# Gated mix of an FFT filter and a Mish MLP on one core: other queues and slices for the first loads, and a new order of the tasks

## The chip, the cores and the metric

The kernel runs on one core of a Trainium2 chip. The metric is the device time of one execution in microseconds (us): before, 133.72 us in the median of three runs (133.17 to 134.02). The core has five engines with queues of their own: TensorE (PE; its weight loads are listed as PEld), VectorE (DVE), ScalarE (ACT), GpSimd (POOL) and SyncE (SP), which only issues transfers. Transfers are issued by SP and ACT, each on a queue of its own, and are carried by 16 shared DMA engines.

## The reference, cut to what matters

```python
x = A_x                                            # 1 x 2048 x 512, bf16
g = sigmoid((x * gate_w).sum(-1, keepdims=True))
X = rfft2(x) * (A_w_r + 1j * A_w_i)                # filter: 2048 x 257, two parts
a = irfft2(X)
h = x @ w1 + b1                                    # w1: 512 x 1792, the same x
act = h * tanh(softplus(h))                        # Mish
b = act @ w2                                       # w2: 1792 x 512
return g * a + (1 - g) * b
```

Two branches read the same x: a two-dimensional Fourier filter, and an MLP with the Mish function. A gate for each row mixes them.

## The kernel before, in words

x is kept as 16 tiles of 128 rows. The program is a list of named tasks, each with its engine and what it reads and writes; a string, ORDER, gives the order of the tasks on each engine (`name:engine:slot`, where the slot is a bank of PSUM for PE's tasks, or a scratch buffer). Every engine works through its own tasks in that order and waits by semaphore for what a task needs. A task that waits holds up all that is behind it on its engine. Tasks that two numbers name belong to a chunk (four tiles of x) or a tile and a part.

The tasks, by the stage they belong to:

- Loads. `x0`, `x2` (two tiles each, 256 KB), `x4`, `x8`, `x12` (four tiles, 512 KB); `w1_0`, `w1_2`, `w1_6`: slices of w1 by columns (2, 4 and 8 of the 14 column tiles of 128); `gw`: the gate weights, one row read 128 times into all partitions; `cRF`, `cFD`, `inv`, `rft`, `edge`, `ldM0..3`, `ldG0..3`: constants of the Fourier stages; `braw`: the bias; `w2_*`: slices of w2. `wr..s..` and `wi..s..` (for instance `wr0s1`): the rows of the filter into a staging area, in ten loads, each into 16 partitions; of each half one load takes 32 rows as they lie, one takes 31 or 32 rows in reversed order, and for the first half one takes a single row.
- PE warm-up. `warm` (14 matmuls of 256 columns on constants) and the fillers `fl0`, `fl1`, `fl2` (3, 8 and 5 matmuls of 128 columns, whose results nobody reads).
- `tr`: transposes a tile of x on PE; `evx` evicts it (ACT or DVE). `tr_b`, `ev_b`: the same for the bias.
- `bf` (DVE): sums and differences of the halves of x. `p`, `d`, `t`, `it`, `id`, `ip`: the matrix stages of the forward and inverse transform on PE; `ep`, `ed`, `et`, `eit`, `ec`, `ey` evict them. `sh` and `hx` are copies between the stages, inside SBUF.
- `gt` (DVE): the gate's dot product, one for each tile, with `gw`; `zcl`, `ez`, `ez1`, `omg`, `gc`: the sigmoid.
- `wrm`, `wim`, `win`, `wrn`, `wrc`, `wic`, `wrz`, `wiz`: bring the filter from the staging area into its final place (mostly DVE). `p2`, `p1`, `ad` (DVE): multiply by the filter. `e1`, `xp2`, `xp1`, `ead`, `e2`, `e3`: a correction for the edge frequencies between the filter and the inverse transform; all of `it` comes after `e3`.
- `m<chunk>_<ft>` (mm1): four matmuls of 512 columns into one PSUM bank; `h<chunk>_<ft>` (ACT): Mish of it. `n<tile>` (mm2): 14 matmuls into one bank. `o` and `s`: scale and add the two branches into the result; `out`: stores. The last tile, 15, is made in two halves of 256 columns.

A PSUM bank is taken again only when its last reader is done. mm1 of chunk 0 needs `evx0` to `evx3` and a slice of w1; mm1 and mm2 need nothing of the Fourier branch, so ORDER strews them between its stages. The lines of the profile: L463 is the helper that issues every transfer, L475 the one that evicts; L488 warm-up, L498 fillers, L544 `tr`, L567 `p`, L581 `d`, L666 `t`, L740 `it`, L764 `id`, L799 `ip`, L788 mm1, L792 Mish, L815 mm2, L557 `bf`, L589 `gt`, L630 and L631 `wrm`/`wim`, L699 `e1`, L804 and L805 `o`, L809 `s`. Tensors: rA holds x at first, w_sb are w1, w2 and small constants kept in w2's place, rS is the staging area of the filter, ps is PSUM.

Of the kernel before, what the change touches and what calls it, by code (L numbers as in the profile page):

```python
# [309 lines left out]
bf8_1:dve gt4:dve m0_11:pe:3 h0_11:act m1_8:pe:6 h1_8:act tr11:pe:7 evx11:act m0_7:pe:2  # L310
h0_7:act m1_10:pe:6 h1_10:act bf12_1:dve tr9:pe:7 evx9:dve p8:pe:0 p9:pe ep8:act
m0_9:pe:2 tr8:pe:3 p10:pe:4 bf12_0:dve p11:pe p12:pe:0 p13:pe p14:pe:6 p15:pe
h0_9:act ep10:act ep12:act gt5:dve ep14:dve m1_6:pe:2 h1_6:act m0_10:pe:4 h0_10:act
d6:pe:0 evx8:dve gt6:dve gt7:dve gt8:dve d7:pe tr10:pe:2 d4:pe:6 d5:pe
tr12:pe:3 m1_12:pe:4 evx12:dve ed3:act gt9:dve m0_13:pe:5 ed2:act tr15:pe:3 d2:pe:0
d3:pe h1_12:act h0_13:act ed1:act evx15:dve gt10:dve gt11:dve evx10:act d0:pe:6
d1:pe d14:pe:4 d15:pe m1_11:pe:3 m0_8:pe:0 ed0:act ed7:act m1_0:pe:2 tr14:pe:1
h0_8:act h1_11:act wi0s1:sp wi0s2:sp evx14:act wr0s1:sp wr0s0:sp wr1s1:sp wr1s0:sp
wrm001:dve wrm010:dve gt12:dve gt13:dve gt14:dve wrm100:dve d8:pe:4 d9:pe m0_6:pe:6
m1_9:pe:3 tr13:pe:7 gt15:dve wip0:pool wip1:pool ed4:act h1_0:act h0_6:act evx13:dve  # L320
m0_4:pe:1 d12:pe:4 d13:pe m1_1:pe:2 h0_4:act h1_9:act ed6:act h1_1:act d10:pe:0
d11:pe m1_5:pe:3 ed5:act m1_7:pe:4 wi0s0:sp m2_8:pe:2 m0_12:pe:5 m3_11:pe:0 wi1s1:sp
sh0_3:sp sh0_0:sp wim011:dve sh0_2:sp h1_5:act ldM0:sp wim111:dve wrm000:dve wim100:dve
wrm110:dve wim101:dve zcl:dve sh0_1:sp wim110:dve m3_0:pe:3 wrm011:dve t1_0:pe:6 wrm101:dve
wrm111:act h1_7:act t1_1:pe wim000:dve wim001:dve wim010:dve m3_10:pe:4 et1:act win0:dve
h3_0:act h0_12:act m3_2:pe:1 t0_0:pe:6 t0_1:pe et0:dve wic0:dve win1:dve m3_9:pe:3
m1_13:pe:5 wiz0:dve p20_0:dve:0 p21_0:dve:1 h3_2:act h3_11:act h3_10:act ez:pool ldM1:sp
t3_0:pe:0 t3_1:pe sh1_0:sp sh1_2:sp sh1_3:sp sh1_1:sp h1_13:act et3:act m2_10:pe:4
h2_10:act h2_8:act m2_9:pe:5 h2_9:act h3_9:act m2_12:pe:0 t2_0:pe:6 t2_1:pe m2_6:pe:1
m2_4:pe:3 wrn01:sp wrn00:sp et2:act p20_1:dve p21_1:dve p23_0:dve:2 p23_1:dve h2_4:act  # L330
m3_4:pe:6 ldM3:sp t6_0:pe:4 wrc0:dve wrz0:dve p1_3:dve ez1:dve omg:dve ad_3:dve
p1_1:dve t6_1:pe h2_12:act et6:act p1_0:dve wic1:dve t7_0:pe:2 t7_1:pe m2_7:pe:0
et7:act h2_7:act m2_11:pe:7 ldM2:sp wrn10:sp t5_0:pe:4 wiz1:pool ad_0:dve ad_1:dve
t5_1:pe m2_2:pe:2 h2_2:act et5:act wrn11:sp wrc1:dve m3_3:pe:0 m3_6:pe:3 m2_3:pe:2
t4_0:pe:4 t4_1:pe p27_0:dve:0 wrz1:dve p26_0:dve:1 h3_6:act h3_3:act et4:act m3_7:pe:3
m2_1:pe:0 h2_1:act h2_6:act h2_11:act m3_8:pe:4 m3_12:pe:5 m2_13:pe:1 m3_1:pe:7 p22_0:dve:2
p27_1:dve p22_1:dve p1_7:dve p26_1:dve p1_6:dve ad_7:dve h3_12:act h2_13:act p1_2:dve
p25_0:dve:0 ad_6:dve w2_9:sp w2_4:sp w2_0:sp p24_0:dve:1 n5_0:pe:5 h3_8:act h3_7:act
h3_1:act h3_4:act p25_1:dve p24_1:dve ad_2:dve p1_5:dve ad_5:dve edge:sp ldG0:sp
p1_4:dve ad_4:dve o5_0:dve n6_0:pe:3 o6_0:act h2_3:act e1:pe:5 gc:dve xp20:dve:0  # L340
xp21:dve xp1:dve:1 rft:sp ldG3:sp ead:dve:2 m2_5:pe:6 m2_0:pe:7 h2_5:act h2_0:act
inv:sp ldG1:sp e2:pe:2 m3_13:pe:3 e3:dve ldG2:sp it1_0:pe:0 it1_1:pe eit1:dve
it5_0:pe:4 it5_1:pe h3_13:act eit5:act m3_5:pe:7 h3_5:act it2_0:pe:2 it2_1:pe it7_0:pe:0
eit2:act it3_0:pe:4 it3_1:pe it7_1:pe eit7:act eit3:act n4_0:pe:7 it0_0:pe:0 it4_0:pe:2
it0_1:pe it6_0:pe:4 it6_1:pe it4_1:pe eit6:act eit4:act eit0:dve hx8_0:act hx4_1:act
hx8_1:act o4_0:act hx0_0:act n0_0:pe:6 n2_0:pe:2 n3_0:pe:7 id10:pe:0 id11:pe id8:pe:4
hx4_0:act ec10:dve:0 ey10_1:dve ey10_0:dve id9:pe ec8:act:1 hx12_0:act o2_0:act o0_0:act
ey8_0:dve ey8_1:dve n1_0:pe:3 id6:pe:0 ip9:pe:6 o1_0:act o9:act id4:pe:4 ip10:pe:2
id5:pe id7:pe ec6:act:0 ip8:pe:3 ip11:pe:6 hx0_1:sp hx12_1:sp o3_0:dve o11:dve
ec4:act:1 o8:act n7_0:pe:7 ey6_1:dve ey6_0:dve o10:act ip6:pe:6 ip7:pe:0 ey4_0:dve  # L350
id2:pe:2 ey4_1:dve ip4:pe:1 id0:pe:4 id1:pe id3:pe ec0:act:0 o7_0:act s6:dve
ec2:act:1 s4:dve ey0_0:dve n11_0:pe:6 ey0_1:dve s7:dve ey2_1:dve id12:pe:0 ip0:pe:7
ip5:pe:4 id13:pe n10_0:pe:5 s11_0:dve s5:dve s0:dve ey2_0:dve ip3:pe:4 id14:pe:2
id15:pe ip1:pe:7 ec12:act:0 out5:act out7:act ec14:act:1 ey12_1:dve ey12_0:dve ip12:pe:6
ip2:pe:0 n8_0:pe:1 s1:dve ey14_0:dve ey14_1:dve ip13:pe:7 ip15:pe:2 n9_0:pe:3 s3:dve
s8_0:dve s10_0:dve ip14:pe:1 out11:sp out1:sp s2:dve o12:dve n12_0:pe:6 s12_0:dve
n13_0:pe:0 o13:dve s13_0:dve s9_0:dve o14:dve out13:act o15:act out3:act out9:sp
n15_256:pe:7 n14_0:pe:6 s14_0:dve out14:act s15_256:dve out15_256:sp n15_0:pe:1 s15_0:dve out15_0:act
"""


def _build(nc, A_x, A_w_r, A_w_i, B_x, B_w1, B_b1, B_w2, gate_w, out, XTP=16, LATE=8, NWARM=14,
           W1P=((0, 2), (2, 6), (6, 14)), XP=((0, 2), (2, 4), (4, 8), (8, 12), (12, 16)), SH=2):
    cs = _build_consts()
    d_front = nc.inline_tensor(_bf16_bits(cs["front"]), name="c_front").bitcast(BF)
    d_inv = nc.inline_tensor(_bf16_bits(cs["inv"]), name="c_inv").bitcast(BF)
# [4 lines left out]
    G = _Graph()  # L371
    es = ExitStack()
    with es:
# [100 lines left out]
        def evac(name, o, i, n, reads, writes, cls, engs=("act", "dve"), deps=()):  # L474
            fns = dict(dve=lambda e: e.tensor_copy(out=o(), in_=i()), act=lambda e: e.activation(o(), i(), AF.Copy))  # L475
# [410 lines left out]
```

## Time and profile before

| | |
|---|---|
| median of three runs | 133.72 us |
| the profiled execution: its time | 134.83 us |
| the profiled execution: its span | 133.2 us |
| PE busy | 127.2 us (95%) |
| DVE busy | 87.9 us (66%) |
| ACT busy | 77.4 us (58%) |
| moved by DMA | 20.28 MB, mean 152 GB/s |
| granted TensorE clock | 1.00 throughout |

The span runs from the first instruction to the last; the time of the execution has 1.6 us more around it. All times inside the kernel are counted from the start of the span. Matmuls overlap, so a single one is listed with 379 ns although the next one starts sooner; their rate is read from the chain of waits. In the chain, "issue" is time in which an engine waited for nothing that the profile shows. A row of the waits gives total us, number of times, and the longest.

### The profile page before, as it was taken

Reading aid. Unit: us, or ns where it says so; the run is one execution under the profiler, and the core shown is the slowest. Engines: PE = TensorE matmul, PEld = TensorE weight load, DVE = VectorE, ACT = ScalarE, POOL = GpSimd, SP = SyncE. Lnnn points to the kernel's source line nnn. Section 1 sums busy time; section 2 is a strip of 40 time slices with the busy share of each in tenths; the row PEclk is TensorE's granted clock in tenths of the full one; section 3 lists DMA queues with packets and bytes.
Section 4 is the critical chain, followed back from the end, with each engine's and each line's share of the span. In section 5 each row is a group of like instructions: output and inputs, shape, how many; then the busy total and the mean of one; then the engine's idle time right before and its main releaser. Section 6 shows DMA issues by size and latency. Waiting matters only on the chain.

```text
span 133.2 us, 2246 instructions
## 1 busy us (share of the span) xinstructions
PE 127.2 (95%) x901; PEld 71.5 (54%) x901; DVE 87.9 (66%) x162; ACT 77.4 (58%) x110; POOL 5.4 (4%) x13
## 2 busy tenths in 40 slices
...
GB/s 100 145 351 407 307 205 170 172 56 0 245 270 199 219 229 238 220 259 359 348 316 1 0 0 5 0 241 310 74 9 0 0 58 99 0 162 0 0 236 79
DMA packets 12533, 20.28 MB, mean 152 GB/s; under 512 B 1324, under 2 KB 6956, under 8 KB 12460
## 3 DMA queue, kind: packets, MB, share of 16 engines
...
q14 instruction: 2, 0.02, 0.0%
...
## 4 chain that ended last, share of the span: by engine, by line
PE 58%; DVE 30%; DMA 6%; issue 4%; SPq 1%; DVEq 0%
PE ps L815 32%; PE ps L788 14%; DVE tmp L679 7%; DMA w_sb<-in_B_w_dram 6%; DVE rC L684 4%; DVE rC L687 4%; PE ps L740 3%; PE ps L764 3%; PE ps L799 3%; PE ps L567 2%; DVE w_sb L589 2%; DVE rW L630 2%; DVE rA L630 2%; DVE rA L640 2%; PE ps L544 2%
## 5 line engine op out<-in xcount | busy, mean ns | idle before, releaser
L788 PE MATMUL ps<-rX,w_sb 128*128 128x512 bf16 x224 | 51.9, 379 | 1.7 <-DMA w_sb<-in_B_w_dram 1.7
L788 PEld LDWEIGHTS ps<-rX,w_sb 128*128 128x128 bf16 x224 | 20.8, 98 | 23.3 <-issue 1.9
L815 PE MATMUL ps<-w_sb,hs 128*128 128x512 bf16 x112 | 25.0, 379 | 0.0
L792 ACT ACTIVATE hs<-ps,b1f 128x512 bf16<-128x512 f32 x28 | 18.5, 696 | 3.4 <-PE ps L788 3.2
L815 PEld LDWEIGHTS ps<-w_sb,hs 128*128 128x128 bf16 x112 | 10.8, 98 | 12.4
L475 ACT ACTIVATE rC<-ps 128x1024 bf16<-128x1024 f32 x13 | 13.2, 1031 | 1.2 <-PE ps L567 0.7
L815 PE MATMUL ps<-w_sb,rD 128*128 128x512 bf16 x56 | 12.7, 379 | 0.0
L557 DVE TENSOR_TENSOR rB<-rA 128x1024 bf16<-128x1024 bf16 (+1 forms) x10 | 5.5, 580 | 11.0 <-DMA rA<-in_A_x_dram 11.0
L815 PE MATMUL ps<-w_sb,rS 128*128 128x512 bf16 (+1 forms) x70 | 12.3, 336 | 0.0
L809 DVE SCALAR_TENSOR_TENSOR rX<-ps,omg,rX 128x512 bf16<-128x512 f32 (+1 forms) x9 | 5.9, 689 | 9.3 <-PE ps L815 9.3
L475 ACT ACTIVATE tmp<-ps 128x512 f32<-128x512 f32 x7 | 4.1, 597 | 13.4 <-PE ps L764 13.3
L589 DVE SCALAR_TENSOR_TENSOR w_sb<-rA,w_sb 128x512 bf16<-128x512 bf16 x16 | 11.0, 687 | 0.3
L792 ACT ACTIVATE rD<-ps,b1f 128x512 bf16<-128x512 f32 x14 | 9.1, 698 | 3.1 <-PE ps L788 3.1
L679 DVE TENSOR_TENSOR tmp<-rC,rA 64x1024 bf16<-64x1024 bf16 x16 | 10.6, 686 | 0.4
L804 ACT ACTIVATE rX<-ps,gcol 128x512 bf16<-128x512 f32 x4 | 2.6, 690 | 14.0 <-DVE rX L809 14.0
L774 DVE TENSOR_TENSOR rA<-tmp,ps 128x512 bf16<-128x512 f32 x16 | 10.0, 679 | 0.4 <-ACT tmp L475 0.4
L815 PEld LDWEIGHTS ps<-w_sb,rS 128*128 128x128 bf16 x70 | 6.8, 98 | 5.5
L792 ACT ACTIVATE rS<-ps,b1f 128x512 bf16<-128x512 f32 x14 | 9.0, 696 | 0.7 <-PE ps L788 0.3
L815 PEld LDWEIGHTS ps<-w_sb,rD 128*128 128x128 bf16 x56 | 5.4, 98 | 6.1
L804 ACT ACTIVATE rX<-ps,omg 128x512 bf16<-128x512 f32 x6 | 4.0, 685 | 7.4 <-PE ps L815 5.1
L475 ACT ACTIVATE rD<-ps 128x1024 bf16<-128x1024 f32 x8 | 8.0, 1035 | 0.0
L475 ACT ACTIVATE rF<-ps 128x1024 bf16<-128x1024 f32 x6 | 5.8, 1029 | 2.2 <-PE ps L740 2.2
...
## 6 DMA issues: line engine op xcount, KB each, us to landing
...
rF<-c_m SPq DMA_DIRECT2D x4, 512.0 KB, 6.3
rB<-c_g SPq DMA_DIRECT2D x4, 512.0 KB, 6.1
rA<-in_A_x_dram SPq DMA_DIRECT2D x3, 512.0 KB, 13.9
...
w_sb<-in_B_w_dram SPq DMA_DIRECT2D x2, 512.0 KB, 10.0
```

The costliest lines, as they stand in the source:

```text
L475: fns = dict(dve=lambda e: e.tensor_copy(out=o(), in_=i()), act=lambda e: e.activation(o(), i(), AF.Copy))
L557: return e.tensor_tensor(out=xu[:, a:b_, uv, :], in0=x_sb[:, a:b_, 0:256], in1=x_sb[:, a:b_, 256:512], op=ALU.add if uv == 0 else ALU.subt ...
L589: t_gt.append(dve(f"gt{t}", "gate", "stt", 512, lambda e, t=t: e.scalar_tensor_tensor(out=junk, in0=x_sb[:, t, :], scalar=1.0, in1=gwr, op ...
L630: return e.tensor_copy(out=o_, in_=i_)
L679: return e.tensor_tensor(out=zv(z)[lo], in0=Y[hi, f0:f0 + 8, :], in1=Wi[hi, f0:f0 + 8, 0:128], op=ALU.mult)
L684: return e.tensor_tensor(out=Y[:, f0:f0 + 8, :], in0=Y[:, f0:f0 + 8, :], in1=Wr[:, f0:f0 + 8, 0:128], op=ALU.mult)
L774: return e.tensor_tensor(out=yb[:, t:t + 2, 256 * h:256 * h + 256].rearrange("p t (i e) -> p t i e", e=2), in0=t4(z), in1=o4(bank(b, 1)), ...
L788: ins = e.matmul(bank(b), w1_sb[:, dt_, 128 * ft:128 * (ft + 1)], xT[:, c, dt_, :, :], start=(dt_ == 0), stop=(dt_ == 3))
L792: G.add(f"h{c}_{ft}", "mish", dict(act=lambda e, c=c, ft=ft, b=b: e.activation(hs[c][:, ft, :], bank(b), AF.Mish, bias=b1f[:, ft:ft + 1])) ...
L804: f_a = lambda e: e.activation(o_()[0], o_()[1], AF.Copy, scale=o_()[2])
L809: dve(name, "fin", "psums", hi - lo, lambda e: e.scalar_tensor_tensor(out=bs[:, t, lo:hi], in0=bank(b)[:, 0:hi - lo], scalar=col[:, t:t + ...
L815: ins = e.matmul(bank(b)[:, 0:hi - lo], hs[c][:, ft, 128 * tl:128 * (tl + 1)], w2_sb[:, ft, lo:hi], start=(ft == 0), stop=(ft == NFT - 1))
```

## The change

The gate weights are loaded as one row (`gwl`) into one partition, spread over all partitions by a product with a column of ones on PE (`gwb`), and evicted (`gwe`). w1 comes in slices of 4, 5 and 5 column tiles (`w1_0`, `w1_4`, `w1_9`). The filter loads read their rows in rising order as one line of memory for each partition, and what was reversed on the reading side is reversed on the writing side. Two of the three fillers go. The last tile of the result is made in 384 and 128 columns instead of 256 and 256. ORDER is new: all filter loads are on SP, while `w1_9`, `x12`, `cFD`, `ldM0` to `ldM2` and two `sh` copies are on ACT.

```diff
@@ -295,72 +295,72 @@
@@ ORDER (of the old one the first 9 and the last 2 lines) @@
-FILL = (3, 8, 5, )
+FILL = (3, )
...
-warm:pe:0 wrp0:pool ebase:pool ones:pool wrp1:pool ident:pool cRF:act braw:act x0:sp
-fl0:pe:1 tr0:pe:0 x2:sp w1_0:sp w1_2:sp bf0_0:dve bf0_1:dve bf2_1:dve x4:sp
-tr1:pe:1 gw:act tab:act bf2_0:dve evx1:dve fl1:pe:2 tr2:pe:2 evx0:act tr3:pe:3
-evx2:act tr_b:pe:0 p0:pe:4 p1:pe p2:pe:6 ep0:act evx3:dve ev_b:dve fl2:pe:2
-m0_1:pe:0 m0_0:pe:1 p3:pe w1_6:sp x8:sp x12:sp h0_1:act wi1s0:act wr0s2:sp
-bf4_1:dve bf4_0:dve m0_3:pe:0 m0_2:pe:4 m0_5:pe:5 ep2:act h0_0:act h0_2:act tr5:pe:1
-h0_3:act evx5:act tr6:pe:4 evx6:dve tr4:pe:6 tr7:pe:7 evx7:act cFD:sp evx4:dve
-p4:pe:2 p5:pe p6:pe:0 p7:pe h0_5:act ep6:act m1_4:pe:7 m1_3:pe:6 h1_3:act
-gt0:dve ep4:dve gt1:dve gt2:dve m1_2:pe:2 gt3:dve h1_2:act h1_4:act bf8_0:dve
...
-n13_0:pe:0 o13:dve s13_0:dve s9_0:dve o14:dve out13:act o15:act out3:act out9:sp
-n15_256:pe:7 n14_0:pe:6 s14_0:dve out14:act s15_256:dve out15_256:sp n15_0:pe:1 s15_0:dve out15_0:act
+warm:pe:0 cRF:act wrp0:pool ebase:pool ones:pool wrp1:pool ident:pool braw:act x0:sp
+bf0_1:dve fl0:pe:1 tr0:pe:0 bf0_0:dve x2:sp gwl:act tab:act bf2_0:dve evx0:act
+tr1:pe:1 evx1:act tr2:pe:2 tr3:pe:3 gwb:pe:0 p0:pe:4 evx2:act gwe:act bf2_1:dve
+evx3:dve w1_0:sp x4:sp w1_4:sp x8:sp p2:pe:6 p3:pe p1:pe tr_b:pe:2
+ev_b:dve gt0:dve gt1:dve gt2:dve m0_2:pe:2 m0_0:pe:3 bf4_0:dve tr4:pe:0 ep2:act
+ep0:act h0_2:act evx4:dve bf4_1:dve tr5:pe:2 m0_3:pe:4 tr7:pe:5 tr6:pe:0 h0_0:act
+w1_9:act evx5:act gt3:dve x12:act cFD:act evx6:act p4:pe:6 p5:pe p6:pe:2
+p7:pe ep6:act gt4:dve m0_7:pe:1 h0_7:act m0_4:pe:0 h0_4:act evx7:dve m1_4:pe:5
+gt5:dve tr9:pe:1 m1_0:pe:0 h0_3:act evx9:act h1_4:act h1_0:act bf8_0:dve bf8_1:dve
+p8:pe:2 m1_5:pe:1 h1_5:act p9:pe ep4:dve m1_11:pe:0 m1_8:pe:1 p10:pe:4 tr11:pe:6
+p11:pe h1_11:act ep8:act gt6:dve gt7:dve gt8:dve ep10:act m0_6:pe:0 wi0s0:sp
+wr0s1:sp bf12_0:dve bf12_1:dve p12:pe:2 p13:pe h1_8:act h0_6:act p14:pe:4 p15:pe
+ep14:act m1_9:pe:7 wi0s2:sp wr0s0:sp wr0s2:sp gt9:dve evx11:dve h1_9:act ldM1:act
+tr12:pe:0 ldM0:act evx12:act m1_1:pe:1 h1_1:act ep12:dve d2:pe:2 d4:pe:4 d3:pe
+m1_13:pe:7 d5:pe wrm001:dve h1_13:act gt10:dve ed1:dve ed2:dve m1_6:pe:0 h1_6:act
+wr1s1:sp wr1s0:sp d10:pe:2 d0:pe:6 d1:pe wi1s0:sp d11:pe ldM2:act ed5:act
+d6:pe:4 d7:pe tr15:pe:0 m0_8:pe:1 wrm011:dve evx15:dve ed0:dve wi1s1:sp wi0s1:sp
+ed3:act h0_8:act m1_2:pe:2 d14:pe:4 m0_11:pe:3 sh0_2:act gt11:dve wrm101:dve gt12:dve
+d15:pe ed7:act m1_7:pe:1 tr8:pe:0 h0_11:act sh0_1:act h1_2:act tr10:pe:6 wrm000:dve
+wrm111:dve m1_10:pe:7 tr13:pe:3 d8:pe:4 d9:pe evx13:act ed4:act evx8:dve gt13:dve
...
+h3_3:act h3_4:act t1_0:pe:2 t1_1:pe m2_6:pe:5 m3_9:pe:4 m2_0:pe:0 m3_13:pe:1 sh1_0:sp
...
+et4:act w2_4:sp w2_0:sp n2_0:pe:1 h3_1:act omg:dve p24_0:dve:2 h3_11:act o2_0:act
+n4_0:pe:3 h3_2:act m2_10:pe:2 p24_1:dve ad_5:dve p27_1:dve p1_7:dve p1_4:dve ad_4:dve
+edge:sp ad_7:dve e1:pe:1 xp20:dve:0 xp21:dve xp1:dve:1 o4_0:dve inv:sp n6_0:pe:4
...
+ip11:pe:5 ip12:pe:4 n12_0:pe:6 ip0:pe:2 o12:act s13_0:dve s7:dve o11:dve s3:dve
+s0:dve out1:act ip2:pe:1 ip5:pe:7 s5:dve s2:dve out3:act out7:sp n15_0:pe:3
+ip14:pe:1 n8_0:pe:7 s11_0:dve s15_0:dve s12_0:dve out15_0:sp out13:sp s8_0:dve out5:act
+o14:act out9:act out11:act n14_0:pe:6 s14_0:dve out14:act n15_384:pe:7 s15_384:dve out15_384:sp
...
-           W1P=((0, 2), (2, 6), (6, 14)), XP=((0, 2), (2, 4), (4, 8), (8, 12), (12, 16)), SH=2):
+           W1P=((0, 4), (4, 9), (9, 14)), XP=((0, 2), (2, 4), (4, 8), (8, 12), (12, 16)), SH=2):
...
@@ -511,7 +511,7 @@
         dma("cRF", RF, d_front[:, 0, :], kb=32, writes=["cRF"])
         dma("braw", brw, B_b1.rearrange("(ft p) -> ft p", p=128), kb=4, writes=["braw"])
         dma("cFD", FD.rearrange("p c m -> p (c m)"), d_front[:, 1:5, :].rearrange("p c m -> p (c m)"), kb=128, writes=["cFD"])
-        dma("gw", gwr, gate_w.unsqueeze(0).to_broadcast([128, 512]), kb=128, writes=["gw"])
+        dma("gwl", junk[0:1, :], gate_w.unsqueeze(0), kb=1, writes=["gwl", "junk"])
         for a, b_ in XP:
             dma(f"x{a}", x_sb[:, a:b_, :], xv[:, a:b_, :], kb=128 * (b_ - a), writes=[("x", t) for t in range(a, b_)])
         for a, b_ in W1P:
@@ -522,14 +522,17 @@
                 sg = stg[64 * ri + 32 * fh:64 * ri + 32 * fh + 32]
                 c0_ = 1 - fh
                 parts = [(0, slice(0, 32), slice(32 * fh, 32 * fh + 32), 257),
-                         (1, slice(c0_, 32), slice(127, 96, -1) if fh == 0 else slice(96, 64, -1), 514)]
+                         (1, slice(31, 0, -1) if fh == 0 else slice(31, None, -1), slice(97, 128) if fh == 0 else slice(65, 97), 514)]
                 if fh == 0:
                     parts.append((1, slice(0, 1), slice(64, 65), 8))
                 for j, (pm, fs, ms, kb) in enumerate(parts):
-                    dma(f"{nm}{fh}s{j}", sg[pm:32:2, fs, :], wv[:, ms, :], kb=kb, writes=[(nm, fh, "s", j)])
+                    dma(f"{nm}{fh}s{j}", sg[pm:32:2, fs, :], wv[:, ms, :].rearrange("q m k -> q (m k)"), kb=kb, writes=[(nm, fh, "s", j)])
         for t in range(XTP, NT):
             dma(f"xt{t}", xT[:, t // 4, :, t % 4, :], xv[:, t, :], queue=("sp",), transpose=True, kb=128, writes=[("xT", t)])
 
+        gb = _Buf("b1")
+        G.add("gwb", "small", dict(pe=lambda e: e.matmul(bank(gb), one[0:1, :], junk[0:1, :], start=True, stop=True)), ("pe", 1, 512), reads=["gwl"], writes=[gb])
+        evac("gwe", lambda: gwr, lambda: bank(gb), 512, [gb], ["gw"], "small")
         bb = _Buf("b1")
         t_trb = G.add("tr_b", "small", dict(pe=lambda e: e.transpose(bankb(bb)[:, 0:14], brw, identt[0:14, 0:14])), ("pe", 1, 14), reads=["braw", "ident"], writes=[bb])
         dve("ev_b", "small", "psum", 14, lambda e: e.tensor_copy(out=b1f[:, :], in_=bankb(bb)[:, 0:14]), reads=[bb], writes=["b1f"])
@@ -818,9 +821,9 @@
                 if late:
                     G.add(f"ip{t}", "ip", t_ip, ("pe", 1, 512), reads=[("yb", t, 0), ("yb", t, 1), "rft"], writes=[b])
                     first(f"o{t}", b, 0, 512, gcol, "gc", bsk)
-                for lo, hi in ([(0, 256), (256, 512)] if t == NT - 1 else [(0, 512)]):
+                for lo, hi in ([(0, 384), (384, 512)] if t == NT - 1 else [(0, 512)]):
                     b2 = _Buf("b1")
-                    keys = [("bs", t, h) for h in (0, 1) if lo <= 256 * h < hi]
+                    keys = bsk if t < NT - 1 else bsk[:1] if lo == 0 else bsk[1:]
                     G.add(f"n{t}_{lo}", "mm2", dict(pe=lambda e, b2=b2, lo=lo, hi=hi, f_mm2=f_mm2: f_mm2(e, b2, lo, hi)), ("pe", NFT, hi - lo),
                           reads=[("hs", c, ft) for ft in range(NFT)] + [("w2", ft) for ft in range(NFT)], writes=[b2])
                     (second if late else first)(f"{'s' if late else 'o'}{t}_{lo}", b2, lo, hi, omg, "omg", keys)

```

More of the change, by code (lines that the diff above doesn't have):

```diff
@@ L307 @@
-h0_3:act evx5:act tr6:pe:4 evx6:dve tr4:pe:6 tr7:pe:7 evx7:act cFD:sp evx4:dve
-p4:pe:2 p5:pe p6:pe:0 p7:pe h0_5:act ep6:act m1_4:pe:7 m1_3:pe:6 h1_3:act
-gt0:dve ep4:dve gt1:dve gt2:dve m1_2:pe:2 gt3:dve h1_2:act h1_4:act bf8_0:dve
[L310 to L356, printed above, removed]
```

30 lines of the change are left out of this document (added).

## The prediction

> **What bounds the kernel now.** I read the busy shares first.
>
> ```profile
> PE 127.2 (95%) x901; PEld 71.5 (54%) x901; DVE 87.9 (66%) x162; ACT 77.4 (58%) x110; POOL 5.4 (4%) x13
> ```
> TensorE (PE) is occupied for 127.2 of 133.2 us. So time can be won only where PE waits, or does work that nobody needs. The chain that ended last (start, length, what) says where.
>
> ```profile
> 1.71 7.49 DMA w_sb<-in_B_w_dram
> 9.19 0.14 issue
> 9.33 1.89 PE ps L788 x8
> 14.03 0.89 PE ps L544 x16
> 15.81 4.36 PE ps L788 x20
> ...
> 118.95 12.14 PE ps L815 x70
> 131.08 0.02 issue
> 131.11 0.48 DVE rX L809
> ```
> The load of the first w1 slice ends at 9.19 and the first matmul group of mm1 starts at 9.33. From there PE runs nearly unbroken to 131.08; the tail is one eviction and one store. An mm1 token (four 512-column matmuls) costs 4 x 4.36/20 = 0.87 us, a token of four 128-column matmuls (tr, p, d, t, it, id) 4 x 0.89/16 = 0.22, and a mm2 group of 14 matmuls 14 x 0.218 = 3.05. The waits (engine, line, for whom: total us, times, longest) name PE's holes after the start.
>
> ```profile
> PE ps L788 <- DMA w_sb<-in_B_w_dram: 1.7, 1, 1.7
> PE ps L699 <- DVE rX L805: 0.7, 1, 0.7
> PE ps L544 <- DMA rA<-in_A_x_dram: 0.6, 1, 0.6
> PEld ps L788 <- ACT hs L792: 0.2, 1, 0.2
> ```
> 1.7 us for w1, 0.6 for the second x slice, and 0.7 at L699 (e1), where the bank is still being evicted by VectorE (DVE). A bank that ScalarE (ACT) frees too late costs one 0.2 us on the weight-load side only. What the transfers did in the meantime stands in the windows (us; busy by engine; clock, DMA share and GB/s are last) and in the DMA issues (KB each, median us to landing).
>
> ```profile
> 0.00:3.33 3.33, 2.49 (x12) 1.76 (x13) 0.00 (x0) 0.96 (x1) 1.29 (x9) 1.00 0.36 100
> 3.33:6.67 3.34, 2.74 (x36) 2.21 (x34) 1.65 (x5) 1.55 (x4) 0.00 (x0) 1.00 0.52 145
> 6.67:10.00 3.33, 1.60 (x21) 1.10 (x19) 0.62 (x3) 1.19 (x2) 0.00 (x0) 1.00 0.98 353
> 10.00:13.30 3.30, 3.30 (x20) 1.65 (x19) 1.29 (x2) 2.39 (x4) 0.00 (x0) 1.00 1.05 401
> 13.30:16.70 3.40, 3.40 (x41) 2.50 (x40) 2.19 (x6) 3.40 (x6) 0.00 (x0) 1.00 1.05 309
> 16.70:20.00 3.30, 3.30 (x17) 1.47 (x15) 3.23 (x9) 2.55 (x5) 0.00 (x0) 1.00 1.25 205
> 20.00:25.00 5.00, 5.00 (x56) 3.57 (x55) 3.14 (x8) 4.82 (x8) 0.00 (x0) 1.00 1.13 183
> ```
> ```profile
> w_sb<-in_gate_w_dram ACTq DMA_DIRECT2D x1, 128.0 KB, 6.8
> rS<-in_A_w_i_dram ACTq DMA_DIRECT2D x1, 257.0 KB, 6.5
> rS<-in_A_w_r_dram SPq DMA_DIRECT2D x3, 257.0 KB, 12.0
> rA<-in_A_x_dram SPq DMA_DIRECT2D x3, 512.0 KB, 13.9
> out_dram<-rX SPq DMA_DIRECT2D x1, 64.0 KB, 1.6
> ```
> Three stages: slow at first (100 and 145 GB/s), then full (353 and 401) while whole-partition x and w1 slices pass, then slow again (309, 205, 183) while the filter rows pass. The gate-weight broadcast needs 6.8 us for 128 KB, and lies over it. DVE shows when x slices came:
>
> ```profile
> 1.97 0.37 ACTq L463 DMA_DIRECT2D w_sb<-in_gate_w_dram  x1
> 5.79 0.76 DVE L557 TENSOR_TENSOR rB<-rA 128x512 bf16<-128x512 bf16 x2 [0.93 <-DMA rA<-in_A_x_dram]
> 12.01 1.29 DVE L557 TENSOR_TENSOR rB<-rA 128x1024 bf16<-128x1024 bf16 x2 [4.72 <-DMA rA<-in_A_x_dram]
> 22.14 0.69 DVE L557 TENSOR_TENSOR rB<-rA 128x1024 bf16<-128x1024 bf16 x1 [1.24 <-DMA rA<-in_A_x_dram]
> ```
> x2 is there at 5.79, x4 at 12.01, x12 at 22.14; the broadcast was issued at 1.97, so it was under way until about 8.8.
>
> **The change, part by part.** *Gate row instead of broadcast, and w1 slices of 4, 5, 5.* In front of the first mm1 stand, on SyncE's queue (SP), x0 and x2 as before, then a w1 slice of 512 KB instead of 256. After x2 (5.76) 512 KB take 3.6 us at 145 GB/s (landing 9.4) and 1.5 us at 353 (7.2). The low rate was measured under the broadcast, which is now one row of 1 KB; so I lean to the fast end: 7.8, first mm1 1.5 us earlier. Bounds: +0.2 (9.4 and the 0.14 us of issue) and -1.8, since ev_b must have freed m0_2's bank, behind four p tokens and tr_b, which I put at 7.5. The added matmul (gwb, 0.22) and the removed fillers lie in that wait; its eviction (gwe) on ACT costs 0.6, as do the others of 512 elements, while m0_2 is still waiting. Without that cover the two would cost 0.8.
>
> p3 moves ahead of the first mm1, into the wait: -0.2.
>
> *x4, w1_4, x8* follow on SP: 1664 KB at 401 GB/s are 4.25 us, so x8 lands at 12.05. PE wants x4 at tr4, 1.74 us after the first mm1 (two mm1 tokens): 9.5, against a landing of 9.1. w1_4 (10.8) is wanted at m0_7 (12.1), x8 at tr9 (14.9). None stalls, with 0.4 us to spare at the tightest.
>
> *w1_9, x12 and cFD go to ACT's queue*, behind h0_2 and h0_0, which wait for the first two mm1 tokens; ACT reaches them near 10.5 to 12.5. Queued behind them on ACT are evx5, evx6 and ep6, so issuing (three times about 0.5 us, by the 0.37 above and longer ones) delays these a little: m0_4 then waits for evx6 about 0.2, counted below. Meanwhile SP, which waits for nothing here, has all ten filter loads behind x8. Both queues then share the DMA engines from 12.05 on. Wanted are: w1_9 at m1_11, which stands behind 8 mm1 and 11 short tokens from the first mm1, 7.8 + 6.96 + 2.42 + 0.3 of small waits = 17.5; x12 at bf12_0 so early that bf12_0 and bf12_1 (0.65 each, from 1.29 for two) are done when PE comes to p12, three mm1 and three short tokens later, 20.8: so 19.5. At 257 GB/s (the middle of 309 and 205), with 60% to ACT's queue, 640 KB land at 16.3 and 1152 KB at 19.7. Cost 0.2. Bounds: 0 (309 GB/s throughout), and 4 us, worked out under the second rival.
>
> *Filter rows in one line.* The reversed half is now read as one run and reversed on the SBUF side; the bytes stay. The trace shows no such load. wrm001 needs the first five filter loads, 779 KB, beside ACT's 1280: at 257 GB/s all are there at 20.3, at 183 at 23.6; DVE comes to wrm001 near 23.3. Queued behind it on DVE stand ed1 and ed2, for whose banks d10 and d0 wait on PE, so lateness here stalls PE at once. Cost 0, bounds 0 and 0.3; below nothing is excluded, as nobody waits for filters earlier.
>
> *The new order in the middle.* ldM0 to ldM2 and two of the sh copies move to ACT's queue; they are issued earlier, ahead of a need that comes at 41 or later, beside the rest of the filters: nothing. e1 takes a bank that ACT, not DVE, evicted (o2_0), and DVE does as much before xp20 as now: three ed evictions (1.2 each) and one wrm more, an et, an evx, an o and two small ones less, about +1.8 us, against three gt (0.73 each) pulled into its idle stretch before x4 (4.7 us). So the 0.7 us hole at L699 mostly closes: -0.6; bounds 0 and -0.7. Against that the new order uses banks more tightly. I walked the new PE and ACT queues side by side, with these rows for a Mish and its result:
>
> ```profile
> L475 DVE CAST rC<-ps 128x1024 bf16<-128x1024 f32 x3 | 3.7, 1222 | 0.9 <-PE ps L567 0.9
> L589 DVE SCALAR_TENSOR_TENSOR w_sb<-rA,w_sb 128x512 bf16<-128x512 bf16 x16 | 11.0, 687 | 0.3
> L475 ACT ACTIVATE rX<-ps 128x512 bf16<-128x512 bf16 x7 | 4.2, 602 | 1.8 <-PE ps L544 1.8
> L792 ACT ACTIVATE hs<-ps,b1f 128x512 bf16<-128x512 f32 x28 | 18.5, 696 | 3.4 <-PE ps L788 3.2
> L788 PE MATMUL ps<-rX,w_sb 128*128 128x512 bf16 x224 | 51.9, 379 | 1.7 <-DMA w_sb<-in_B_w_dram 1.7
> ```
> A bank is free again 0.16 (379 ns of a matmul less its 218 ns slot) + 0.70 + 0.1 us after its last slot. m1_0 comes into bank 0 1.09 us after m0_4 left it, with h0_7 ahead of h0_4 on ACT; such places (m0_4, m1_0, m1_11, m1_6, d0, m2_0) cost 0.1 to 0.4 each: +0.85; bounds 0, as in the trace of before, and 1.4.
>
> *The last block in 384 and 128 columns.*
>
> ```profile
> 129.58 1.14 DVE L809 SCALAR_TENSOR_TENSOR rX<-ps,omg,rX 128x512 bf16<-128x512 f32 x2 [2.48 <-PE ps L815]
> ```
> PE now ends with 14 matmuls of 128 columns (0.78 us) over which s14 (0.75) runs; the last eviction has half the width, 0.34 instead of 0.48 (0.27 of the 0.75 belong to 256 columns). The store still takes 1.6. So -0.15; bounds 0 and -0.2.
>
> Sum: -1.5 - 0.2 + 0.2 - 0.6 + 0.85 - 0.15 = -1.4 us. Against the profiled execution (span 133.2, its time 134.83, so 1.6 us lie around it) that is a span of 131.8; that execution was 1.1 us above the median 133.72, and I subtract from the median: **132.3 us**. Its own range, from the bounds without the rivals' cases: 131.2 to 133.4.
>
> **The rivals.** *First: the first w1 slice comes no earlier.* If the early rate is the queues' start and not the broadcast, 512 KB land at 9.4: +0.2 instead of -1.5, so 134.0. For it: the first window (100 GB/s) is slow too, before the broadcast. Against it: 353 GB/s are reached just as the broadcast ends.
>
> *Second, the other side: the filter loads hold up w1_9.*
>
> ```profile
> 10.39 0.63 ACTq L463 DMA_DIRECT2D rS<-in_A_w_i_dram  x1
> ```
> One filter load was issued on ACT's queue at 10.39 and landed 6.5 us later, while those on SP's took 12.0 and x slices 13.9: a queue of its own gets turns, whatever is queued on the other. Now the long rows are on SP and the short ones on ACT. If a turn is one row, a filter row of some 16 KB goes for each 1280-byte piece of w1_9, and w1_9 waits for nearly all filters: 2056 KB at 257 GB/s from 12.05 is 20.2, then 640 KB at 401 give 21.8. m1_11 is wanted at 17.5, and all of PE stands behind it: +4.3, less the 0.2 already counted: 136.4. It decides from w1_9 landing after 17.5 or x12 after 19.5; with equal shares x12 lands at 21.2, and it costs 1.7 (133.8). The Trainium skill speaks for it: "DMA: Bandwidth & Descriptors", section Queues, rings and completion order, says that each DMA engine goes round the queues packet by packet. By that rule the sum would be this rival's; the 6.5 us agree that turns are taken, but no run here shows what a turn holds when rows are long on one side. The same page, section Issuing engines are not separate DMA queues, adds that a second queue brings no bandwidth; the sum above gives it none.
>
> *Third: one line does nothing.* If the reversed rows still move row by row, filters pass at 183 GB/s, wrm001's come at 23.6 and cost 0.3: 132.6.
>
> *Fourth: the clock.* Without fillers PE is idle a little longer before the first mm1.
>
> ```profile
> 0.84 3.14 PE L488 MATMUL ps<-const-bfloat16-1.0 128*128 128x256 bf16 x14 [0.84 <-PEq L871]
> ```
> The warm-up shows the slow state: 14 matmuls of 256 columns in 3.14 us, 0.22 each, what 512 columns take later. Fallen back for about as long, PE would lose half of 3.1 us: 133.9. The holes are near 1 us (x2) and below; before, one of 1.7 us (L788) was followed at once by full-speed matmuls, so I hardly believe it. The Trainium skill ("TensorE: Matmul & The Clock Gate", Part 1) asks for an idle window of about 3.4 us; this trace agrees, with its 1.7.
>
> **How the numbers follow.** The forecast gets 0.52, the first rival 0.15, the second 0.26 (0.05 of it with equal shares), the third 0.04, the fourth 0.03. 1% is 1.34 us, about what a measurement of this kernel can tell from no change: faster means below 132.4, slower above 135.1. The forecast lies on that edge; most of what its bounds add is downward (a wait that closes wholly, banks that cost nothing), so of its 0.52 I count 0.42 faster and 0.10 within 1%. Within 1% also fall the first, third and fourth rivals and the equal shares: 0.10 + 0.15 + 0.04 + 0.03 + 0.05 = 0.37; the rest of the second, 0.21, is slower. The range starts at 131.1, and to leave out no more than 2 in 10 it reaches to 135.9, into the second rival, which ends past it if the filters go entirely first.
>
> **What would show it.** Right: the first wait of PE at L788 for w_sb ends near 7.9 instead of 9.33; early windows above 200 GB/s; the chain without L699 waiting for DVE; small PE waits for ACT below 0.4 us each; 1.9 to 2.0 us from the last matmul to the end. Wrong: a wait of PE or DVE for w_sb or rA between 17 and 24 us (second rival), for rS at L630 (third), the first mm1 after 9.3 (first), or a PE wait above 1 us anywhere after 25 us, for which this sum has no term.

## The result, and the profile after

The changed kernel takes 141.67 us (median of 4 runs, 141.12 to 142.65) against 133.87 before on the same chip: 1.059 times as long, 95% interval 1.050 to 1.068. The forecast was 132.3 with a range to 135.9: wrong in sign, and outside the range. The second rival names the load and the place; even its 136.4 is 5 us short. (The profiled execution of after is the 142.65 one.) Below, a time is the median of all executions of a run, and a ratio compares only those in the chip's faster state with those of before on the same chip, so the two need not agree exactly. Behind L530 the changed kernel's lines stand three lower: mm1 is L791, the Mish L795, `tr` L547, `p` L570, `d` L584, `bf` L560; L534 is `gwb`, L538 `ev_b`.

Busy time and instructions by engine, and the clock in 40 slices (tenths of full speed):

```profile
PE 129.7 (92%) x889; PEld 71.9 (51%) x889; DVE 96.7 (68%) x169; ACT 70.2 (50%) x103; POOL 6.1 (4%) x14
PEclk9999975579999999999999999999999999999999
```
TensorE (PE) issues 12 instructions fewer than before and is busy 2.5 us longer, and four slices between 18 and 32 us run at 5 to 7 tenths of the clock. PE's waits (total, times, longest), and VectorE's (DVE) for x:

```profile
PE ps L791 <- DMA w_sb<-in_B_w_dram: 7.8, 1, 7.8
PE ps L488 <- PEq L874: 0.8, 1, 0.8
PE ps L791 <- ACT rS L795: 0.5, 1, 0.5
PE ps L791 <- DVE b1f L538: 0.3, 1, 0.3
DVE rB L560 <- DMA rA<-in_A_x_dram: 14.2, 4, 9.1
```
One wait for w1 costs 7.8 us; the wait at e1 (L699 before, L702 now) is gone from the list; the first mm1 now waits for ev_b, not for w1. DVE waits 9.1 us for x12. The chain (start, length, what):

```profile
9.92 15.36 DMA w_sb<-in_B_w_dram
25.41 3.57 PE ps L791 x8
28.99 0.43 PE ps L570 x4
...
32.78 0.22 PE ps L547 x4
...
132.45 6.84 PE ps L818 x42
139.31 0.35 DVE rX L812
```
w1_9, issued by ScalarE (ACT) at 9.92, lands 15.36 us later. The eight matmuls behind it then take 3.57 us, 0.45 each; a short token takes 0.43 at 28.99 and 0.22 again at 32.78. By stage (us; busy of PE, PEld, DVE, ACT, POOL; clock, DMA share, GB/s):

```profile
3.33:6.67 3.34, 3.13 (x27) 2.33 (x25) 1.88 (x5) 2.12 (x6) 0.00 (x0) 1.00 0.94 291
6.67:10.00 3.33, 3.06 (x30) 1.88 (x29) 2.26 (x9) 3.15 (x5) 0.00 (x0) 1.00 1.00 365
10.00:13.30 3.30, 3.30 (x38) 2.34 (x37) 3.27 (x10) 2.28 (x4) 0.00 (x0) 1.00 1.24 253
16.70:20.00 3.30, 0.95 (x8) 0.42 (x6) 2.06 (x7) 1.33 (x3) 0.00 (x0) 0.95 0.92 168
20.00:25.00 5.00, 0.00 (x0) 0.00 (x0) 0.00 (x0) 0.00 (x0) 0.00 (x0) 0.50 1.06 252
25.00:30.00 5.00, 4.58 (x21) 2.38 (x22) 2.02 (x5) 1.60 (x2) 0.00 (x0) 0.51 0.50 97
30.00:35.00 5.00, 5.00 (x50) 3.25 (x48) 3.16 (x6) 4.73 (x7) 0.00 (x0) 1.00 0.24 47
```
The front went as forecast (291 GB/s where 145 stood). From 20 to 25 us no engine works while the DMA engines are full, and the clock is at half speed until 30. Who had the DMA engines? The queues (q1 is SyncE's (SP), q10 ACT's; packets, MB, share) from 10 to 16 us, then from 20 to 23:

```profile
DMA packets 1047, 1.23 MB, mean 205 GB/s; under 512 B 90, under 2 KB 951, under 8 KB 1016
q1 hardware_dynamic: 1047, 1.23, 112.4%
```
```profile
q10 hardware_dynamic: 358, 0.47, 70.0%
q1 hardware_dynamic: 353, 0.24, 39.6%
```
Until 16 us SP's queue has everything: not one packet of w1_9 in the six us after its issue. From 20 on the two take turns packet by packet. So of w1_9's 15.4 us 6.1 pass before its first packet (at 16.02), and 9.3 in turns with the filter rows.

### The profile page after: what moved, and what is told of

Read it like the earlier page. It is cut to its first block, busy times and chain, and to the rows that moved or that the text cites. A ratio compares the mean times of both kernels' runs of the same rounds, so it can differ in the third digit from the quotient of the medians.

```text
span 141.4 us, 2218 instructions
## 1 busy us (share of the span) xinstructions
PE 129.7 (92%) x889; PEld 71.9 (51%) x889; DVE 96.7 (68%) x169; ACT 70.2 (50%) x103; POOL 6.1 (4%) x14
## 2 busy tenths in 40 slices
DMA packets 12392, 20.16 MB, mean 143 GB/s; under 512 B 1437, under 2 KB 7326, under 8 KB 12318
## 4 chain that ended last, share of the span: by engine, by line
PE 73%; DMA 14%; DVE 5%; POOL 2%; ACT 2%; issue 2%; SPq 0%; DVEq 0%; POOLq 0%
PE ps L818 34%; PE ps L791 23%; DMA w_sb<-in_B_w_dram 11%; DMA rA<-in_A_x_dram 3%; PE ps L743 3%; PE ps L584 3%; PE ps L767 3%; PE ps L802 2%; POOL ez L597 2%; PE ps L547 2%; PE ps L570 2%; PE ps L669 1%; ACT rC L475 1%; ACT rS L795 1%; DVE rA L643 1%
## 5 line engine op out<-in xcount | busy, mean ns | idle before, releaser
L791 PE MATMUL ps<-rX,w_sb 128*128 128x512 bf16 x224 | 55.0, 388 | 8.5 <-DMA w_sb<-in_B_w_dram 7.8
L791 PEld LDWEIGHTS ps<-rX,w_sb 128*128 128x128 bf16 x224 | 20.8, 99 | 29.9 <-issue 9.6
L795 ACT ACTIVATE hs<-ps,b1f 128x512 bf16<-128x512 f32 x28 | 18.3, 690 | 11.8 <-PE ps L791 11.6
L818 PEld LDWEIGHTS ps<-w_sb,hs 128*128 128x128 bf16 x112 | 10.8, 98 | 12.3
L475 ACT ACTIVATE rC<-ps 128x1024 bf16<-128x1024 f32 x14 | 14.1, 1029 | 2.3 <-PE ps L570 1.8
L560 DVE TENSOR_TENSOR rB<-rA 128x1024 bf16<-128x1024 bf16 (+1 forms) x10 | 5.5, 581 | 14.2 <-DMA rA<-in_A_x_dram 14.2
L795 ACT ACTIVATE rD<-ps,b1f 128x512 bf16<-128x512 f32 x14 | 9.2, 688 | 7.3 <-PE ps L791 7.2
L818 PE MATMUL ps<-w_sb,rS 128*128 128x512 bf16 (+2 forms) x70 | 12.8, 336 | 0.0
L812 DVE SCALAR_TENSOR_TENSOR rX<-ps,omg,rX 128x512 bf16<-128x512 f32 (+2 forms) x9 | 6.1, 690 | 5.9 <-PE ps L818 5.5
L475 ACT ACTIVATE tmp<-ps 128x512 f32<-128x512 f32 x6 | 3.3, 595 | 12.4 <-PE ps L767 12.4
L818 PEld LDWEIGHTS ps<-w_sb,rS 128*128 128x128 bf16 x70 | 6.3, 98 | 6.0 <-DVE rX L812 0.3
L795 ACT ACTIVATE rS<-ps,b1f 128x512 bf16<-128x512 f32 x14 | 8.9, 684 | 0.7 <-DVE rA L634 0.6
L475 DVE CAST rF<-ps 128x1024 bf16<-128x1024 f32 x5 | 5.9, 1221 | 1.9 <-PE ps L743 1.9
L547 PE MATMUL ps<-identt,rA 128*128 128x128 bf16 x64 | 6.4, 245 | 0.2 <-DMA rA<-in_A_x_dram 0.2
L812 DVE SCALAR_TENSOR_TENSOR rX<-ps,gcol,rX 128x512 bf16<-128x512 f32 x8 | 5.8, 745 | 0.9 <-PE ps L802 0.9
```

What stands on the lines that cost most here:

```text
L547: ins = e.transpose(bankb(b)[:, 128 * dt_:128 * (dt_ + 1)], x_sb[:, t, 128 * dt_:128 * (dt_ + 1)], identt[:, :])
L560: return e.tensor_tensor(out=xu[:, a:b_, uv, :], in0=x_sb[:, a:b_, 0:256], in1=x_sb[:, a:b_, 256:512], op=ALU.add if uv == 0 else ALU.subt ...
L791: ins = e.matmul(bank(b), w1_sb[:, dt_, 128 * ft:128 * (ft + 1)], xT[:, c, dt_, :, :], start=(dt_ == 0), stop=(dt_ == 3))
L795: G.add(f"h{c}_{ft}", "mish", dict(act=lambda e, c=c, ft=ft, b=b: e.activation(hs[c][:, ft, :], bank(b), AF.Mish, bias=b1f[:, ft:ft + 1])) ...
L812: dve(name, "fin", "psums", hi - lo, lambda e: e.scalar_tensor_tensor(out=bs[:, t, lo:hi], in0=bank(b)[:, 0:hi - lo], scalar=col[:, t:t + ...
L818: ins = e.matmul(bank(b)[:, 0:hi - lo], hs[c][:, ft, 128 * tl:128 * (tl + 1)], w2_sb[:, ft, lo:hi], start=(ft == 0), stop=(ft == NFT - 1))
```

## The experiments

### What the loads on ACT's queue cost

*a_sp*: the three loads back on SP's queue.

```diff
-... w1_4:sp x8:sp p2:pe:6 ... w1_9:act evx5:act gt3:dve x12:act cFD:act evx6:act
+... w1_4:sp x8:sp w1_9:sp x12:sp cFD:sp p2:pe:6 ... evx5:act gt3:dve evx6:act
```


> The changed kernel with w1_9, x12 and cFD on SyncE's queue right behind x8 and ahead of the filter rows, nothing else moved. Theory Q (the filter rows on SyncE's queue starve the three loads on ScalarE's): the eight loads are 3.84 MB in line, w1_9 lands near 16.5 us and x12 near 18.4 us, the 7.8 us stall ahead of m1_11 and the half clock behind it are gone, filters end 2 to 4 us later than 30.8; 133 us (131.5 to 136). Theory O (the new order itself is the loss, the stall only hides it): 138 us or more. Theory B (the bytes, not the queue: 5.9 MB in 30 us are too many in any order): w1_9 early but the filters late by as much, 139 us or more.

132.38 us, 0.991 of before (0.987 to 0.995). PE's waits, and the busy times:

```profile
PE ps L547 <- DMA rA<-in_A_x_dram: 0.9, 1, 0.9
PE ps L488 <- PEq L874: 0.8, 1, 0.8
PE ps L791 <- ACT rS L795: 0.5, 1, 0.5
PE ps L791 <- DVE b1f L538: 0.3, 1, 0.3
PE 126.6 (97%) x889; PEld 70.3 (54%) x889; DVE 96.3 (73%) x169; ACT 70.1 (53%) x103; POOL 6.1 (5%) x14
```
Same bytes, same order elsewhere, and the loss is gone: the placement of the three loads is the cause, as theory Q has it; O and B fall. Which company on SP's queue does it, this run can't tell. The placement of three loads costs 1.0588 - 0.9909 of 133.9, some 9 us.

*a_hold*: the three loads stay on ACT, but every filter load waits for x12 (`deps=[t_x]`).

> The changed kernel with every filter load held on SyncE until x12 has landed; w1_9, x12 and cFD stay on ScalarE's queue. Theory Q: with no filter packets beside them w1_9 lands within 6 us of its issue at 9.9 us and x12 by 19 us, no stall at m1_11, filters end near 33 us; 133.5 us (132 to 137). Rival S (ScalarE's queue is slow by itself, or w1_9 is issued too late): w1_9 lands at 20 us or later though no filter moves, 138 us or more.

133.38 us, 0.993 (0.989 to 0.997). The two loads (KB, us from issue to landing):

```profile
w_sb<-in_B_w_dram ACTq DMA_DIRECT2D x1, 640.0 KB, 4.5
rA<-in_A_x_dram ACTq DMA_DIRECT2D x1, 512.0 KB, 5.4
```
4.5 us instead of 15.4 for w1_9. It was issued at 11.6, when SP's queue was all but empty (x8 landed at 12.4), and moved its first packet 1.1 us later. So ACT's queue isn't slow by itself; S falls.

*a_early*: the same three loads on ACT, issued near 2.2 us instead of 9.9.

> The changed kernel with w1_9, x12 and cFD still on ScalarE's queue, but issued near 2.2 us, ahead of its first evictions. Theory Q with the filter rows as the cause: these loads share the engines with x4, w1_4 and x8, not with filter rows; w1_9 lands near 12 us, x4 and w1_4 up to 2 us later than in a_sp; 133.5 us (132.3 to 136). Rival P (ScalarE's queue always yields to SyncE's): w1_9 lands at 20 us or later, 139 us or more.

134.05 us, 1.001 (0.997 to 1.005). w1_9 is there at 11.1, w1_4 at 13.96, for which PE waits 1.5 us. From 8 to 10 us, with x and w1 pieces on both queues:

```profile
q1 hardware_dynamic: 253, 0.40, 52.1%
q10 hardware_dynamic: 260, 0.39, 51.1%
```
Equal turns; P falls. The Trainium skill ("DMA: Bandwidth & Descriptors", Queues, rings and completion order) has each DMA engine go round its queues packet by packet. These rows agree, as do those from 20 to 23 us above; the six us in which ACT's queue got no turn aren't explained by that rule. Nor does a first wait need filter rows: here w1_9's first packet came at some 5.6 us, 3.3 after its issue, while the first filter load was given out only at 4.54. From 4 to 5.5 us the queues moved:

```profile
q1 hardware_dynamic: 343, 0.37, 95.3%
q10 hardware_dynamic: 9, 0.00, 0.6%
```

*a_w1only*: w1_9 alone goes back to SP.

> The changed kernel with w1_9 alone moved to SyncE's queue behind x8; x12 and cFD stay on ScalarE's, beside the filter rows. Theory Q (any load on ScalarE's queue waits behind the filter rows): w1_9 lands near 13.6 us as in a_sp, no wait at m1_11; x12 issued near 9.9 us lands at 24 us or later, and the matmul that needs it (at 20.8 us in a_sp, behind 1.3 us of VectorE) waits some 5 us, with a half clock of up to 1 us behind it; 138.5 us (137 to 140.5). Rival A (the three loads only hold up one another; one alone is quick): x12 by 20 us, 133 us.

135.21 us, 1.011 (1.002 to 1.019): between the two, and outside both theories. x12, issued at 9.94, lands at 21.36 (11.4 us), and PE waits 2.4 us, not 5, at full clock in the profiled execution. x12 is held there too, but for less long.

### Half clock

*a_fill*: 120 small matmuls ahead of m1_11 (`FILL = (3, 120, )`, `fl1:pe:0 m1_11:pe:0`).

> The changed kernel with 120 small matmuls on a constant ahead of m1_11, 6.7 us of idle work inside the 7.8 us stall. Theory C (about 2 us of the loss is the half clock that follows the idle TensorE): clock 0.9 or more from 20 to 30 us, w1_9 as late as before, 139.5 us (139 to 140.3). If the half clock costs nothing, because the filters and the forward stage are late anyway: 141.7 us.

140.70 us, 1.051 (1.044 to 1.058): 0.008 of 133.9, 1.1 us, less than the changed kernel, where 2.2 were expected. (The two intervals overlap, so the 1.1 is known only to within about 1 us.) The chain shows what came next:

```profile
10.21 17.66 DMA rA<-in_A_x_dram
27.90 1.31 DVE rB L560 x2
29.25 1.07 PE ps L570 x16
```
At full speed PE comes sooner to the tokens that need x12, which is late as well. So part of the cost of the slow clock, half by these medians, lay beside that second lateness.

### Which filter rows hold the queue

*a_rowold* reads the mirrored rows as before, `wv[:, slice(127, 96, -1), :]`, with queues as changed.

> The changed kernel with the mirrored filter rows read as before, row by row in reverse, queues and order as changed. Theory Q needs only that filter rows are on SyncE's queue beside the loads on ScalarE's: w1_9 still near 25 us, 141.7 us (141 to 142.5). Rival L (reading the rows in one line is what makes the turns long): w1_9 by 20 us, 136 us or less.

142.38 us, 1.061 (1.052 to 1.070), w1_9 15.0 us from issue to landing. L falls. *d_long* holds the mirrored rows until x12 is there (`deps=[t_x] if j else []`), *d_rev* the forward ones (`deps=[] if j else [t_x]`), and *d_short* has each forward load as two, of `slice(0, 32, 2)` and `slice(1, 32, 2)`.

> The changed kernel, w1_9, x12 and cFD on ScalarE's queue. SyncE issues the four forward filter loads (64 rows of 16448 bytes) first, as early as before; the mirrored ones (rows of 514 bytes) are held until x12 has landed. Theory R (the 16448-byte rows are what holds ScalarE's queue): 4 rows on each engine of 1.1 to 1.5 us, w1_9 near 20 us, stall of some 2.5 us, 136 us (134.5 to 138). Theory N (the some 2000 short rows of SyncE's queue, given out ahead of w1_9, are what holds it): w1_9 at 16 to 17.5 us as in a_hold, 133.5 us (132.5 to 134.5).

> The reverse: the mirrored filter loads (some 2000 rows of 514 bytes) are issued early, the four forward ones are held until x12 has landed. Theory R: no long row beside w1_9, turns of 514 against 1280 bytes: w1_9 by 18 us, 134 us (132.5 to 135.5). Theory N: w1_9 at 22 us or later, 137 us or more.

> The changed kernel with each forward filter load in two, of the even and the odd rows, so that no row longer than 514 bytes is left and some 4000 short ones are; nothing held. Theory R: w1_9 by 18 us, 135 us or less. Theory N: twice the rows ahead of w1_9, w1_9 at 25 us or later, 141 us or more.

| filter rows not held | w1_9, issue to landing | of it, to its first packet | longest wait of PE for w1 | time | ratio to before |
|---|---|---|---|---|---|
| long and short (after) | 15.4 us | 6.1 us | 7.8 us | 141.67 us | 1.059 |
| long only (d_long) | 12.3 | 4.7 | 4.2 | 138.54 | 1.025 (1.018 to 1.033) |
| short only (d_rev) | 12.2 | 4.0 | 4.1 | 139.08 | 1.032 (1.024 to 1.039) |
| short only, twice as many in all (d_short) | 13.8 | 4.7 | 5.2 | 140.37 | 1.044 (1.038 to 1.050) |
| none (a_hold) | 4.5 | 1.1 | none | 133.38 | 0.993 |

(On the chip of the three d runs before takes 134.73 us. The profiled execution of d_long is the longest of its four, 139.84.)

Both theories missed: R by d_rev and d_short, N by d_long and d_short. d_short is no clean test of twice the rows: when w1_9 was issued at 9.76, SP had given out five of its fourteen filter loads, some 1300 short rows against some 2000 in d_rev. Either kind does about half of the harm. In all three ACT's queue moves nothing from 10 to 14 us; d_rev, then d_long, in that window:

```profile
q1 hardware_dynamic: 1090, 0.86, 117.8%
```
```profile
q1 hardware_dynamic: 196, 1.07, 113.7%
```
In a_hold, where w1_9 is issued 1 to 2 us later than there, it moved 144 packets in it.

Yet the first wait isn't peculiar to filter rows. The kernel before had it too: its filter load on ACT's queue, issued at 10.39, moved its first packet at 14.5, 4.1 us later. From 10 to 14 us SP's queue moved packets of x and w1, all but 37 of them between 2 and 8 KB:

```profile
DMA packets 655, 1.61 MB, mean 403 GB/s; under 512 B 32, under 2 KB 37, under 8 KB 655
q1 hardware_dynamic: 655, 1.61, 104.8%
```
In the d runs x8 was still under way (it lands at 15.1 to 16.0), so their first 4.0 to 4.7 us can't be put down to filter rows alone. What the filter rows beside w1_9 do show is the time from its first packet to landing: 7.6 to 9.3 us with them, 5.5 beside x and w1 (a_early), 3.5 without company. What decides when a queue gets its first turn behind loads given out earlier on the other stays open.

### The parts that were meant to gain

*b_gate*: the kernel before with the gate row alone (`gwl`, `gwb:pe:3`, `gwe:dve`).

> The kernel before with the gate weights as one row, a product on TensorE and an eviction on VectorE in place of the broadcast load; nothing else. Theory G (the broadcast's small packets keep w1_0 back): w1_0 lands by 7.5 us instead of 9.2, the first mm1 starts near 7.8 us instead of 9.3, and the 1.5 us reach the end: 132.4 us (131.7 to 133.3). Rival H (later loads are no earlier, so the gain is given back as waits): 133.9 us.

132.53 us, 0.993 (0.990 to 0.996). The chain has no DMA left in front:

```profile
6.77 0.32 PE ps L534
7.09 0.40 PE ps L498 x5
7.49 1.73 PE ps L791 x8
```
*c_gate*: a_sp with the broadcast put back.

> a_sp with the broadcast load of the gate weights put back. Theory G: w1_0 lands near 9.2 us instead of 6.9, the first mm1 starts 1.5 us later, 133.9 us (133.3 to 134.8). If the new order gains by itself: 132.9 us or less.

133.27 us, 0.996 (0.993 to 0.999): between G and its alternative. G's account of the front doesn't hold here: w1_0 lands at 8.02, and the first mm1 starts at 8.16 against 7.86 in a_sp, 0.3 later and not 1.5. By the medians the gate row is worth 0.9 us on the old order and (0.996 - 0.991 of 133.9) 0.7 on the new; the second is not clear of noise, as the intervals of c_gate and a_sp overlap.

*b_w1*: the kernel before with `W1P=((0, 4), (4, 9), (9, 14))` alone.

> The kernel before with w1 in slices of 4, 5 and 5 tiles instead of 2, 4 and 8, in the same places of the queue. By the bytes: w1_0 is 256 KB longer and lands 0.7 us later, w1_4 about 0.4 us later, x8 and x12 1 us earlier; 133.9 us (133.3 to 134.8).

134.40 us, 1.006 (1.003 to 1.009): a loss of 0.8 by itself, within the range but not the 0.2 of the bytes. w1_0 landed at 8.77, not later but 0.4 us earlier than the one of half the size before (9.19); it has as many rows, each twice as long. The profile shows no wait of PE that is over 0.1 us longer than before's, so the loss is not explained.

*c_row*: a_sp with the old reading of the mirrored rows.

> a_sp with the mirrored filter rows read row by row as before. If reading in one line changes nothing on the chip (packets of the reversed rows stay 514 bytes): filters end at 28.7 us give or take 1, 132.4 us (131.9 to 132.9). If it makes the filters quicker: they end 2 us later without it, 133 us or more.

132.56 us, 0.992 (0.988 to 0.996). The page counts the same packets in both; this is its row in c_row, and, word for word but for the rate, in a_sp:

```profile
DMA packets 12392, 20.16 MB, mean 152 GB/s; under 512 B 1437, under 2 KB 7326, under 8 KB 12318
```
```profile
DMA packets 12392, 20.16 MB, mean 154 GB/s; under 512 B 1437, under 2 KB 7326, under 8 KB 12318
```
Reading in one line doesn't make longer packets; no effect on the time can be told.

*c_tail*: a_sp with the last block in halves, `[(0, 256), (256, 512)]`.

> a_sp with the last block in halves of 256 and 256 columns instead of 384 and 128. By the rows of the two profiles the last eviction is 0.13 us shorter at 128 columns; the last product is the same work: 132.5 us, 0.15 us more than a_sp (0 to 0.4 more).

132.71 us, 0.992 (0.989 to 0.994): not to be told from a_sp. From the end of PE's last matmul to the end of the span it is 2.10 us in a_sp and 2.15 in c_tail.

*c_best*: a_sp with two waits taken away.

```diff
-p1:pe tr_b:pe:2 ... m3_8:pe:7 win0:dve wic0:dve wiz0:dve p20_0:dve:0 wim111:dve
+p1:pe tr_b:pe:1 ... m3_8:pe:7 wim111:dve win0:dve wic0:dve wiz0:dve p20_0:dve:0
```


> a_sp with two more edits: the filter move wim111 goes ahead of win0, wic0, wiz0 and p20_0 on VectorE, and the bias transpose tr_b goes into bank 1, so that the first mm1 (bank 2) no longer waits for its eviction. In a_sp these waits were 0.5 us (mm1 for the Mish held by the last filter move) and 0.3 us. Theory W (both waits lie on TensorE's path, nothing else is late behind them): 131.6 us (131.2 to 132.0). Rival V (the next wait takes their place): 132.4 us.

132.09 us, 0.9885 (0.984 to 0.993), between W and V: the best median here, though its interval overlaps a_sp's. Its waits:

```profile
PE ps L584 <- DVE rD L475: 0.9, 1, 0.9
PE ps L488 <- PEq L874: 0.8, 1, 0.8
PE ps L547 <- DMA rA<-in_A_x_dram: 0.2, 1, 0.2
```
Both waits are gone; in the profiled execution (133.41, the longest of its six) a d token waited 0.9 for its bank, behind filter loads that came later than in a_sp.

## Why the prediction was wrong

- **The step that failed** is "with 60% to ACT's queue, 640 KB land at 16.3 and 1152 KB at 19.7. Cost 0.2." It took both queues as moving side by side from 12.05 on, and w1_9 as done 4.25 us later. Measured: no packet until 16.0, then 9.3 us in turns with the filter rows; w1_9 at 25.3, x12 at 27.9; the term was some +9 us (a_sp).
- **Second rival**: right on the side and on the place (m1_11 waits for w1_9 beside the filter rows), too small in price, 21.8 for the landing. It had no wait ahead of the first turn, and it let all filter bytes pass at 257 GB/s, where 168 were measured from 16.7 to 20 us. The row that was quoted for quick turns, 6.5 us for a filter load on ACT's queue, was misread: 4.1 of the 6.5 passed without a packet of it. So "a queue of its own gets turns, whatever is queued on the other" was not what the trace of before showed.
- **Fourth rival**: I looked for a fall of the clock in the front only. It came behind the 7.8 us wait: 1.1 us by a_fill. "A PE wait above 1 us" should have carried this price with it. The Trainium skill ("TensorE: Matmul & The Clock Gate", Part 1) puts the fall after an idle window of about 3.4 us. The lengths of the waits agree in the profiled executions: full clock behind 2.4 us (a_w1only), 0.75 of it from 20 to 25 us around a wait of 4.1 (d_rev), half behind 7.8. The moment doesn't: in the changed kernel PE's last matmul ahead of the wait ended at 17.7, and the clock was 1.00 from 18 to 19.6 us and 0.59 from 19.6 to 20, so it fell some two us into the wait.
- **First mm1, -1.5**: right in size. It starts at 7.97 instead of 9.33, held by ev_b as bounded; in b_gate at 7.49. The first rival is out: w1_0 lands at 6.78. But the reason was only partly right: in the new order the broadcast costs the front 0.3 (c_gate). And to the end of the kernel the gate row brings 0.7 to 0.9 us, not 1.5.
- **Wait at L699, -0.6**: right, it is gone. In its place came one of 0.5 us, for which the sum had no term: the Mish results go into the staging tile rS, and wait for the last filter move, wim111, which the new order puts behind p20_0.
- **Tight banks, +0.85**: too high. a_sp shows no wait of PE for a bank beyond the 0.3 for ev_b and that 0.5.
- **Last block, -0.15**: 0.05 by the profiles of a_sp and c_tail. The last eviction went from 0.48 to 0.35 as worked out, but the store behind it takes 1.7 us for 32 KB where it took 1.6 for 64.
- **One line**: the third rival is right on the packets, but nothing was waiting for them: c_row is no slower.

With the queue placement undone, the rest of the change is worth 1.2 us (0.7 to 1.7); the sum without its ACT term said 1.6. That the two are near is partly luck, for the terms err in both directions: the first brings less at the end than at the front, the slices of w1 lost 0.8 by themselves on the old order (b_w1), and the banks cost less than the 0.85.
